# Rows of a half block in a free buffer of attention's weights, and pieces of blocks between the last group's transposes

## The chip, the cores and the metric

The kernel runs on one core of a Trainium2 chip. The metric is the device time of one execution in microseconds. Engines are named as in the profile: PE is TensorE's matmul and PEld its weight load, DVE is VectorE, ACT is ScalarE, POOL is GpSimd, SP is SyncE, which here issues most of the loads.

## The reference

Two layers stand one behind the other. The first is attention that keeps the 32 largest scores of each query; the second sends each token to one of eight experts (a dropless mixture).

```python
# q, k, v: (8, 8, 576, 64)
scores = scale * np.matmul(q, k.transpose(0, 1, 3, 2))
kth = np.partition(scores, -top_k, axis=-1)[..., -top_k:-top_k + 1]   # top_k = 32
scores = np.where(scores >= kth, scores, -1e9)
attn = np.exp(scores - np.max(scores, axis=-1, keepdims=True))
attn = attn / (np.sum(attn, axis=-1, keepdims=True) + 1e-09)
x = np.matmul(attn, v)            # then (B,H,S,D) -> (4608, 512)

logits = x @ w_gate               # (512, 8)
expert_idx = np.argmax(logits, axis=1)
gate_w = softmax(logits)[arange(N), expert_idx]
# tokens sorted by expert; for each expert e with rows lo:hi
h = np.maximum(x_sorted[lo:hi] @ w1[e], 0.0)      # w1: (8, 512, 1024)
y_sorted[lo:hi] = h @ w2[e]                       # w2: (8, 1024, 512)
return gate_w[:, None] * y_sorted[inv_perm]
```

All of it is float32.

## The kernel before

**Attention.** The eight batches come one after the other, each as four pairs of heads. Two neighbouring pairs make nine groups of two query tiles each, so a batch has 18 groups and the kernel 144. For a group, PE multiplies the scores (`products`, L292), ACT copies them out, DVE searches the threshold (`search`), ACT and POOL mask and ACT takes the exponential (`depths`, `less`, `weights`). The result is a tile "w" of 128 partitions by two times 576 numbers, in a pool of three buffers. `transposed` then turns it on PE: four transposes into a PSUM bank "wTm" for each of the group's two tiles (L415), each copied out by ACT to "wT" (L422), and one more "wTl" for the rest (L429), copied to "wTt" (L437). `transposed` is a generator: it stops after the copies and after "wTl", and `loop` puts other work of PE at these stops. For the last group of all, nothing is put there. `outputs` multiplies the turned weights by the values (po, L450), then turns the result into rows and logits (px, L461).

**Routing.** When a batch is done, DVE chooses the experts, PE counts ranks (L531 to L534), and POOL scatters the rows to their expert's place in a DRAM tensor `x_rows` (L567). At the last batch SP and POOL also write blank rows behind the filled ones (`fill_up`, L589), and DVE works out a table that says which block belongs to which expert.

**Blocks.** A block is 128 sorted rows of one expert. `load_rows` fetches its rows to a tile "xg" (L769; four buffers in all, 514 numbers a row: 512 of x, one of the gate, one index), `load_weights` its expert's w1 (L761) and w2 (L763, two buffers each), all on SP's queue. `turned` transposes the rows on PE (xtp, L808), the first layer is 32 matmuls, each of which stands twice in the profile (ph, L913), ACT applies the relu (L918), the second layer is eight matmuls of 512 columns, also twice each (py, L930). ACT scales by the gate (L939), and `put_rows` sends the rows to their tokens in the output by an indirect DMA of POOL (L828), which reads index and gate from the "xg" tile. That store is the last reader of the tile.

A long block has 192 rows: 128 in one "xg" tile and a half of 64 in another (`load_half`, L782). There are four of them, `HALVES`, all in the last part. Their transposes are L798, the first layer is L849, the second L870 (both in PSUM tiles that the program calls "sc"), the turning back of the result L885, and the scaling L889. The rooms for their turned rows and hidden numbers come from the pool "s", attention's scores. A long block's output is turned back and stored in the middle of the next block's first layer (`finish`).

**Order.** A block is cut into 16 pieces: eight of four first-layer matmuls and eight of one second-layer matmul. `pieces(n)` issues the next n of them, going on to the next loaded block where one ends; when a block is begun, `ahead` issues the loads of the one two behind it. Inside `loop` the order on PE, ACT and DVE is the program's own. Three blocks' worth of pieces, `KEEP`, are kept back and issued after the last group, to cover the routing of the last batch. What comes after that, the first two sure blocks, the four long ones and the four plain ones, is ordered by a planner that goes by its own costs; SP's and POOL's queues are ordered by it everywhere.

The end of `loop` before the change, after all 144 groups:

```python
            for _ in turning(len(work) - 1):
                pass
            assert len(late) == 1
            clock = None
            for place in late[0][0]:
                if place == "rows":
                    pieces(4)
            kept = left - (SURE + HALVES + PLAIN) * PIECES
            ...
            pieces(kept)
```

`late[0]` is the ending of the last pair of heads: outputs, routing, tables and loads, in steps.

Of the kernel before, what the change touches and what calls it, by code (L numbers as in the profile page):

```python
# [9 lines left out]
F32 = mybir.dt.float32  # L10
# [20 lines left out]
def _turned(ap: bass.AP, axis: int) -> bass.AP:  # L31
    dims = [list(d) for d in ap.ap]
    step, n = dims[axis]
    dims[axis] = [-step, n]
    return bass.AP(tensor=ap.tensor, offset=ap.offset + step * (n - 1), ap=dims)
# [7 lines left out]
def kernel(  # L43
# [48 lines left out]
    B, U, P, _ = qk.shape  # L92
    N, Dm = out.shape
    S = N // B
# [14 lines left out]
    XW = Dm + 2  # L109
# [20 lines left out]
    k = SimpleNamespace()  # L130

    def open_pools(st, exact):
        for name, bufs in (
            ("load", 2), ("att", 2), ("xp", 1 if exact else 2), ("small", 2),
            ("wp", 1 if exact else 2), ("mlp", 2),
        ):
            setattr(k, name, st.enter_context(tc.tile_pool(name=name, bufs=bufs)))
        for name, bufs in (("ps_s", 2), ("ps_t", 2), ("ps_m", 2)):
            pool = tc.tile_pool(name=name, bufs=bufs, space=bass.MemoryType.PSUM)
            setattr(k, name, st.enter_context(pool))  # L140
        k.exact = exact
        k.apart = False

    def load_unit(b, u, parts=False):
        n = SimpleNamespace(b=b, u=u)
# [107 lines left out]
    def bank(name):  # L253
        return k.ps_t.tile([P, SM], F32, name=name, tag="t")
# [8 lines left out]
    def tails(tiles):  # L263
        return tiles[0][1] == 2 * NC

    def tail_at(n):
        return 0 if n.u % 2 else S
# [140 lines left out]
    def transposed(tiles, w):  # L408

        q = slice(ST + tiles[0][1] * P, ST + (tiles[0][1] + 1) * P)  # L410
        for m, (n, i) in enumerate(tiles):
            pm = bank("wTm")
            for c in range(NC):
                first = c * P + (0 if tails(tiles) else m * ST)
                nc.tensor.transpose(pm[:, c * P:(c + 1) * P], w[:, m, first:first + P], ident)  # L415
            pm4 = pm[:, :].rearrange("p (c q) -> p c q", c=NC)
            if tails(tiles):
                at = tail_at(n)
                pmh = pm4.rearrange("p c (h q) -> p c h q", h=2)
                nc.scalar.copy(wT[:, :, :, at:at + ST], _turned(pmh, 2) if m else pmh)  # L420
            else:
                nc.scalar.copy(wT[:, :, m, q], pm4)  # L422
        yield
        pt = bank("wTl")
        if tails(tiles):
            for a in range(2):
                nc.tensor.transpose(pt[0:ST, a * P:(a + 1) * P], w[:, 1 - a, SM:S], ident)
        else:
            nc.tensor.transpose(pt[:, 0:P], w[:, :, :].rearrange("p m k -> p (m k)")[:, SM:SM + P], ident)  # L429
        yield  # L430
        if tails(tiles):
            pt4 = pt[0:ST, 0:2 * P].rearrange("p (r q) -> p r q", q=ST)
            for h in range(2):
                both = wTt[h * ST:(h + 1) * ST, :].rearrange("p (a q) -> p a q", q=ST)[:, 0:NT + 1:NT, :]
                nc.scalar.copy(both, pt4[:, 0:4:3, :] if h else pt4[:, 1:3, :])
        else:
            nc.scalar.copy(wTt[:, q], pt[:, 0:P])  # L437
# [340 lines left out]

    def load_half(n, piece):
        r = nc.sync.value_load(piece, min_val=0, max_val=EMPTY)  # L780
        n.half = k.mlp.tile([P, 1, XW], F32, name="xg", bufs=4)
        got = nc.sync.dma_start(n.half[0:ST], xv[0:ST, bass.ds(r, 1), :]).ins  # L782
        for put in scattered:
            tc.add_manual_dep(got, put.name, WAIT)
        fetched.append(got)
        return n
# [170 lines left out]
    with fast:  # L957
# [49 lines left out]
        def pieces(n):  # L1007
            nonlocal current, left
            while n > 0 and left > 0:
                if current is None:  # L1010
                    if not landed(loaded[0]):
                        break
                    now = loaded.pop(0)
                    if hasattr(now, "half"):
                        current = long_block(now, following)
                    else:
                        current = block(now, following, stores.append)
                    ahead()
                if clock is None:
                    evacuate()  # L1020
                step = next(current)
                if step == "pause":
                    if clock is not None:
                        break
                    continue
                if step == "last":
                    current = None
                n -= 1
                left -= 1
            return n  # L1030
# [117 lines left out]
        def turning(i):  # L1148
            return transposed(tiles_of(i), w_of.pop(i))
# [9 lines left out]
        def loop():  # L1159
            nonlocal credit, rate, clock  # L1160
            for i in range(min(AHEAD, len(work))):
                multiply(i)
                s_of[i], steps = scores(got_of.pop(i))
                for step in steps:
                    step()
            multiply(AHEAD)
            f_of[0] = fold(s_of[0])
            fold_on(f_of[0])
            for i, (b, g) in enumerate(work):
                tiles = tiles_of(i)  # L1170
                u, tile = g[0]
                if tile == 0 and u % 2 == 0:
                    open_unit(tiles[0][0])
                if tails(tiles):
                    open_unit(tiles[1][0])

                then = lambda: None
                if i + 1 < len(work):
                    f_of[i + 1] = fold(s_of[i + 1])
                    then = lambda: fold_on(f_of[i + 1])  # L1180
                low, nbias, doubts = search(tiles, s_of[i], f_of.pop(i), then)
                at_place("small")
                w_of[i] = depths(s_of[i], low)
                less(s_of.pop(i), w_of[i])
                doubts()
                put_stores()
                scatter(1)
                at_place("pool")
                at_place("relu")
                at_place("rows")  # L1190
                at = i % per_batch
                if at == FIRST and b:
                    rate = level(b) * PIECES / (U * NT)
                credit += rate * len(g)
                room = left
                if b == B - 1 and at >= ARRIVED:
                    room -= KEEP
                    credit = room / (len(work) - i)
                share = {0: 0.5, 1: 1.2, 2: 1.6, 3: 0.5, 2 * NC: 1.4}[tile]
                now = max(0, min(int(credit * share + 0.5), room))  # L1200
                credit -= now
                clock = i
                if i + AHEAD < len(work):
                    s_of[i + AHEAD], steps = scores(got_of.pop(i + AHEAD))
                    for step in steps:
                        step()
                evacuate()
                at_place("turn")
                turns = turning(i - 1) if i else iter(())
                next(turns, None)  # L1210
                part = min(BETWEEN, now - now // 2)
                rest = pieces(part)
                next(turns, None)
                rest = pieces(now - now // 2 - part + rest)
                weights(tiles, w_of[i], nbias)
                next(turns, None)
                evacuate()
                if i + AHEAD + 1 < len(work):
                    multiply(i + AHEAD + 1)
                if tile == NC - 1:  # L1220
                    end = ending(b, u)
                    late.append([end, next(end)])
                at_place("products")
                at_place("weights")
                credit = min(credit + pieces(now // 2 + rest), 6 * rate)

            for _ in turning(len(work) - 1):
                pass
            assert len(late) == 1
            clock = None  # L1230
            for place in late[0][0]:
# [3 lines that stand above are left out]
            assert kept >= 0, kept  # L1235
            k.apart = True
            pieces(kept)
# [20 lines left out]
    with ExitStack() as outer:  # L1258
# [10 lines left out]
        with ExitStack() as st:  # L1269
# [7 lines left out]
            with tc.For_i(0, B, 1) as b:  # L1277
# [3 lines left out]
                for u in range(0, U, 2):  # L1281
# [4 lines left out]
                    for g in groups(u):  # L1286
# [5 lines left out]
                        w = depths(s, low)  # L1292
# [4 lines left out]
                        n, tile = tiles[0]  # L1297
# [76 lines left out]
```

## Time and profile before

| | |
|---|---|
| median of 3 runs | 1328.27 us (1327.86 to 1331.78) |
| the profiled execution | 1330.3 us, its span 1328.6 us |
| busy in the span | PE 1195.5 us (90%), PEld 837.3 (63%), DVE 1073.6 (81%), ACT 933.0 (70%), POOL 657.4 (49%) |
| matmuls of the long blocks (L849, L870) from 1140 to 1314 us | 256 each, 42.8 and 43.4 us busy |
| loads of rows | 37 of 257 KB (L769), 4 of 128.5 KB (L782) |
| loads of expert weights | 74 of 2048 KB |
| granted TensorE clock, 1060 to 1314 us | 1.00 |
| DMA, 1088 to 1156 us and 1156 to 1314 us | share 1.02 at 348 GB/s, and 0.60 at 221 GB/s |

Times in the profile are microseconds from the start of the span. The page divides the span into 40 slices of 33.2 us. A line of the timeline gives the start, the length, the engine and line, what is written and read, and the number of merged instructions; in brackets stands the idle time ahead of it and what ended it. Matmuls follow each other before the one in front has ended, so that the lengths of two neighbours overlap. A line of the waits gives the waiter, what released it, the time in total, the number of waits and the longest. "SPq" is SP's queue.

### The profile page before, as it was taken

What the parts mean: (1) busy time and instruction counts of PE and PEld (TensorE: products, weight loads), DVE (VectorE), ACT (ScalarE), POOL (GpSimd) and SP (SyncE); (2) the same over time, 40 slices, a digit from 0 to 9 for tenths busy, and PEclk for the clock granted to TensorE, in tenths of its full rate; (3) what the DMA queues carried; (4) which work ended last, traced back from release to release, by engine and by line L of the source; (5) the groups of instructions that cost most, each with busy time, mean ns of one, the idle gap of its engine ahead of it and who ended that gap; (6) DMA issues with size and microseconds to landing.
All of it is one profiled execution on the core that took longest, in us unless ns stands there. A gap on an engine that the chain in (4) does not pass through costs nothing. (4 is left out here: it accounts for less than half of the span.)

```text
span 1328.6 us, 24530 instructions
## 1 busy us (share of the span) xinstructions
PE 1195.5 (90%) x7654; PEld 837.3 (63%) x7654; DVE 1073.6 (81%) x4654; ACT 933.0 (70%) x2129; POOL 657.4 (49%) x806
## 2 busy tenths in 40 slices
PE   5767766998889899999999999999999999999995
PEld 3444443666566556676667666766666767799973
DVE  7999999999999999999999999999999942000000
ACT  4888787887898788988888798888878851111210
POOL 2454546564866485647554865576547642000000
PEclk9788788899999899999999999999999999999998
DMA  4000002841293029432954464538354549946780
GB/s 148 30 29 30 30 30 65 311 157 30 72 349 125 30 76 374 172 101 84 367 171 172 137 243 172 173 132 305 134 203 144 208 143 335 347 155 221 291 335 18
DMA packets 98509, 220.95 MB, mean 166 GB/s; under 512 B 5181, under 2 KB 25917, under 8 KB 98368
## 3 DMA queue, kind: packets, MB, share of 16 engines
q1 hardware_dynamic: 91664, 199.02, 42.6%
q0 software_dynamic: 6416, 19.97, 4.2%
q8 instruction: 62, 1.02, 0.3%
q14 instruction: 79, 0.65, 0.1%
q10 hardware_dynamic: 288, 0.30, 0.1%
HBM read 195.88 MB, written 24.17 MB: 166 GB/s over the span
## 5 line engine op out<-in xcount | busy, mean ns | idle before, releaser
L396 POOL TENSOR_TENSOR w<-s,w 128x576 f32<-128x576 f32 x288 | 410.0, 1444 | 417.3 <-ACT w L387 417.3
L913 PE MATMUL ph<-xTs,w 128*128 128x128 f32 x2112 | 260.1, 277 | 3.7 <-ACT xTs L810 3.7
L913 PEld LDWEIGHTS ph<-xTs,w 128*128 128x128 f32 x2112 | 248.7, 192 | 23.2 <-issue 18.6
L930 PE MATMUL py<-w,hT 128*128 128x512 f32 x528 | 250.3, 603 | 2.8 <-ACT hT L918 2.6
L404 ACT ACTIVATE w<-w,nbias 128x576 f32<-128x576 f32 x288 | 224.0, 792 | 4.6 <-POOL w L396 3.9
L387 ACT ACTIVATE w<-s,low 128x576 f32<-128x576 f32 x288 | 207.6, 768 | 4.7
L292 PE MATMUL sc<-qkb 64*128 64x288 f32 (+1 forms) x1280 | 200.0, 463 | 9.5 <-ACT s L299 5.1
L415 PE MATMUL wTm<-turn,w 128*128 128x128 f32 x1152 | 169.4, 287 | 31.9 <-ACT oT L452 14.7
L415 PEld LDWEIGHTS wTm<-turn,w 128*128 128x128 f32 x1152 | 132.0, 145 | 88.3 <-issue 33.4
L299 ACT COPY s<-sc 128x576 f32<-128x576 f32 x288 | 168.7, 639 | 8.3 <-PE sc L292 8.3
L1253 DVE CAST any_i<-pd 1x1 int32<-1x1 f32 x1 | 0.1, 147 | 206.4 <-PE pd L1251 206.4
L354 DVE MAX8 tops<-scr 128x8 f32<-128x168 f32 x576 | 162.9, 317 | 0.0
L422 ACT COPY wT<-wTm 128x512 f32<-128x512 f32 x256 | 139.1, 603 | 23.5 <-PE wTm L415 23.2
L354 DVE MAX8 tops<-few 128x8 f32<-128x144 f32 (+1 forms) x576 | 154.6, 300 | 0.0
L292 PEld LDWEIGHTS sc<-qkb 64*128 64x128 f32 (+1 forms) x1280 | 107.4, 191 | 71.3 <-issue 33.1
L450 PE MATMUL po<-wT,vb 128*64 128x288 f32 x1024 | 149.0, 437 | 0.4 <-ACT wTt L437 0.4
L930 PEld LDWEIGHTS py<-w,hT 128*128 128x128 f32 x528 | 92.7, 193 | 88.4 <-issue 83.8
L828 POOL DMA_INDIRECT out_dram<-y,xg x41 | 41.8, 1020 | 188.3 <-ACT y L889 82.4
L345 DVE MAX8 few<-l 128x8 f32<-128x288 f32 x288 | 127.2, 442 | 0.0
L450 PEld LDWEIGHTS po<-wT,vb 128*64 128x64 f32 x1024 | 72.0, 145 | 72.5 <-issue 22.1
L306 DVE TENSOR_TENSOR h<-s 128x576 f32<-128x576 f32 x144 | 114.0, 792 | 2.6 <-ACT s L299 2.6
L308 DVE TENSOR_TENSOR l<-s 128x576 f32<-128x576 f32 x144 | 110.0, 764 | 0.0
(185 smaller groups left out, 1645.9 us busy)
## 6 DMA issues: line engine op xcount, KB each, us to landing
w<-in_moe_w_dram SPq DMA_DIRECT2D x74, 2048.0 KB
qkb<-in_qk_dram SPq DMA_DIRECT2D x31, 608.0 KB
vb<-in_v_dram SPq DMA_DIRECT2D x32, 320.0 KB
xg<-x_rows SPq DMA_DIRECT2D x37, 257.0 KB
x_rows<-blank SPq DMA_DIRECT2D x13, 257.0 KB
x_rows<-blank POOLq DMA_DIRECT2D x4, 257.0 KB
out_dram<-y,xg POOLq DMA_INDIRECT x41, 2.9
x_rows<-x,posi POOLq DMA_INDIRECT x40, 3.2
```

Of the source, the lines that this page charges most:

```text
L292: nc.tensor.matmul(ps[rows, j, 0:HF], n.q[d, cols], n.k[d, keys], start=True, stop=True)
L299: lambda m=m, ps=ps: nc.scalar.copy(s[:, m, :, :], ps[:, :, 0:HF]) for m, ps in enumerate(got)
L345: nc.vector.max(out=f.few[:, m, QF + 8 * j:QF + 8 * j + 8], in_=away)
L354: nc.vector.max(out=tops[:, m, r * 8:(r + 1) * 8], in_=src[m])
L387: nc.scalar.activation(w[:, m, :], s[:, m, :, :].rearrange("p j k -> p (j k)"), AF.Relu, scale=-STEEP, bias=low[:, m:m + 1],)
L396: k.last_pool = in_turn(nc.gpsimd.tensor_tensor(w[:, m, :], s[:, m, :, :].rearrange("p j k -> p (j k)"), w[:, m, :], op=ALU.subtract)).ins
L404: nc.scalar.activation(w[:, m, :], w[:, m, :], AF.Exp, scale=scale, bias=nbias[:, m:m + 1], accum_out=n.z[:, c:c + 1])
L415: nc.tensor.transpose(pm[:, c * P:(c + 1) * P], w[:, m, first:first + P], ident)
L422: nc.scalar.copy(wT[:, :, m, q], pm4)
L450: nc.tensor.matmul(po[r, 0:HF], n.v[:, c, r], rhs, start=(c == 0), stop=(c == KC - 1))
L913: nc.tensor.matmul(ph[:, f, :], n.w1[:, 0, dt, fc * P:(fc + 1) * P], n.xT[:, dt, :], start=(dt == 0), stop=(dt == DT - 1),)
L930: nc.tensor.matmul(py, hT[:, f, :], n.w2[:, 0, f, :], start=(f == 0), stop=(f == FT - 1))
```

## The change

Two edits, both in the last part. The rows of a half block come into a buffer of the pool of attention's weights "w" (three buffers of 2 times 576 numbers per partition, of which the first 514 are used); before, they came into one of the four "xg" buffers. And in the turning of the last group, one piece of a block is issued at each stop of `transposed`; for this group there is one stop more, behind the copy of the first "wTm", so there are three. These pieces are taken from the same queue of blocks, and what is issued later is as much shorter.

```diff
@@ open_pools
-        k.apart = False
+        k.apart = k.between = False
@@ transposed
             else:
                 nc.scalar.copy(wT[:, :, m, q], pm4)
+                if k.between and not m:
+                    yield
         yield
         pt = bank("wTl")
@@ load_half
         r = nc.sync.value_load(piece, min_val=0, max_val=EMPTY)
-        n.half = k.mlp.tile([P, 1, XW], F32, name="xg", bufs=4)
+        room = k.att.tile([P, 2, S], F32, name="w", bufs=3)[:, :, :].rearrange("p m k -> p (m k)")
+        n.half = room[:, 0:XW].rearrange("p (o w) -> p o w", o=1)
         got = nc.sync.dma_start(n.half[0:ST], xv[0:ST, bass.ds(r, 1), :]).ins
@@ loop
+            k.between = True
             for _ in turning(len(work) - 1):
-                pass
+                pieces(1)
             assert len(late) == 1
             clock = None
```

## The prediction

> **What bounds the kernel now.** I began with the page's slices (each 33.2 us; a digit is the busy share in tenths):
>
> ```profile
> PE   5767766998889899999999999999999999999995
> ...
> DVE  7999999999999999999999999999999942000000
> ```
>
> Until about 1070 us attention's search on DVE is as full as TensorE; from there DVE runs dry and PE alone is full to 1312.9, after which comes a fixed tail of 15.7 us to the span's end at 1328.6. Both edits lie in that last part, so what shortens PE's stream there shortens the kernel one for one. The chain view covers only the end (1299.80 on) and says nothing of this, so next I asked what PE waited for from 1070 on (waiter, line, releaser: us, times, longest):
>
> ```profile
> PE xtp L798 <- DMA xg<-x_rows: 1.7, 4, 0.6
> PE xtp L808 <- DMA xg<-x_rows: 0.7, 1, 0.7
> PE wTm L415 <- ACT wT L422: 0.7, 1, 0.7
> PE wTl L429 <- ACT wT L422: 0.7, 1, 0.7
> PE po L450 <- ACT wTt L437: 0.4, 1, 0.4
> ```
>
> Two clusters: the last group's transposes wait for ScalarE's evacuations, and the long blocks' row transposes wait for their loads. The timeline shows the first (start, length, count, idle before):
>
> ```profile
> 1074.40 1.04 PE L415 MATMUL wTm<-turn,w 128*128 128x128 f32 x8
> ...
> 1078.91 0.66 PE L415 MATMUL wTm<-turn,w 128*128 128x128 f32 x4
> 1080.25 0.66 PE L415 MATMUL wTm<-turn,w 128*128 128x128 f32 x4 [0.68 <-ACT wT L422]
> 1081.58 0.33 PE L429 MATMUL wTl<-turn,w 128*128 128x128 f32 x1 [0.68 <-ACT wT L422]
> 1082.26 2.16 PE L450 MATMUL po<-wT,vb 128*64 128x288 f32 x16 [0.35 <-ACT wTt L437]
> ```
>
> and the second, where the first long block (no wait) stands beside the second:
>
> ```profile
> 1172.27 0.99 PE L798 MATMUL xtp<-turn,xg 128*128 128x128 f32 x8
> 1173.19 10.67 PE L870 MATMUL sc<-s,w 128*128 128x192 f32 x64
> 1183.69 5.36 PE L849 MATMUL sc<-s,w 128*128 128x192 f32 x32
> ...
> 1194.97 0.81 PE L870 MATMUL sc<-s,w 128*128 128x192 f32 x4
> 1196.38 0.66 PE L798 MATMUL xtp<-turn,xg 128*128 128x128 f32 x4 [0.60 <-DMA xg<-x_rows]
> ...
> 1199.23 0.46 PE L798 MATMUL xtp<-turn,xg 64*128 64x64 f32 x4 [0.24 <-DMA xg<-x_rows]
> ```
>
> Why the rows are late is in the waits of SP's queue from 1185 to 1200:
>
> ```profile
> SPq L769 <- DMA out_dram<-y,xg: 43.6, 2, 24.7
> SPq L782 <- DMA out_dram<-y,xg: 2.4, 1, 2.4
> ```
>
> SP stood 24.7 us for a free "xg" buffer, until an old block's output had left it; the load went out at 1193.69 and its transposes began 2.69 us later. Below, A is the block in work at 1079, B to D the kept ones, E and F those before the four long blocks L0 to L3, G the next.
>
> **Part 1: pieces between the last transposes.** It adds no instruction and moves three pieces up. Loss now, start to start: eight wTm take 0.87 us (1074.40, the next matmul at 1075.27), so four take 0.435. 1080.25 - 1078.91 - 0.435 = 0.905 lost; 1081.58 - 1080.25 - 0.435 = 0.895; a lone wTl took 0.10 before matmuls of that kind (1070.86 to 1070.96), so 0.58 before po. In sum 2.38.
>
> What fills it: A has done 14 of its 16 L930 matmuls, so the first piece is its last pair (0.86, 1086.49 to 1087.35), then two pieces of B, whose rows were transposed at 1066.65; eight L913 matmuls take 0.90 (64 of them 7.14: 1103.48 to 1110.62, less a piece's share, 0.89). New order from 1078.91: wTm to 1079.35, piece to 1080.21, wTm at its 1080.25, to 1080.69, piece to 1081.59, wTl to 1081.69, piece to 1082.59, then po, 0.33 later than today but with 2.66 of work done. Gain 2.66 - 0.33 = 2.33. Ends: 1.38 (the idle column 1.71 less the 0.33), and 2.38.
>
> What moves with it. Last outputs and routing start 0.33 later; POOL's chain (L487 to L500), DVE's choice and the scatters shift as much, behind PE's kept work. The four pieces ahead of the ranks stay four; they are now four of B, 3.6 us instead of 3.56. That cover is just enough (the choice ends at 1090.21, its matmul starts at 1090.27), so I put 0 there; without it a late choice costs its lateness. ACT's y of A comes where it came, now without its 0.46 wait for PE; h0 of B is asked for 1.8 us after the px matmuls and done by 2.5, before the Exp of the logits (3.4 after them). On SP, D's loads are issued a little earlier, and w2 of C, which stood for A's last pair until 1087.54, can go at about 1080.3, into a stretch where the DMA engines moved 1 GB/s (1076 to 1088).
>
> **Part 2: halves into "w" buffers.** It removes an "xg" claim from each of L0 to L3; the same 128.5 KB come by the same queue. Loss now against the first long block, whose 64 L870 take 1183.69 - 1173.19 = 10.50 and eight transposes 0.92: L1 runs from 1194.97 to 1207.53, 12.56 for 11.42, so 1.14; L2 from 1218.80 to 1231.41, 12.61, so 1.19; L3 from 1242.68 to 1254.41, 11.73 for 10.96 (four transposes), so 0.77. Sum 3.10. Ends: 2.42, the idle column (0.60 + 0.24 + 0.62 + 0.27 + 0.69), and 3.87, the weight loads' idle column there (0.90 + 0.54 + 0.91 + 0.56 + 0.96). I take 3.10, since the first long block is the nearest row.
>
> What is late next. With four "xg" and rows only, L2's rows take E's buffer (its output issued at 1147.99), L3's F's (1163.03), G's L0's (1190.82, while G's load follows the start of L2 at about 1207): none waits near its use. Three "w" buffers serve L0 to L2 at once, as attention's last transposes end at 1082. L3's half takes L0's and keeps the wait for the store of 1194.34; queued behind it on SP are w1 and w2 of L3 and G's rows. w1 must wait for L1's first half anyhow (1194.97), and is wanted at 1231; 2 MB at the 348 GB/s of 1088 to 1156 take 6 us. So 0. Earlier weights collide with little: from 1156 to 1314 the DMA share is 0.60.
>
> **Sum.** 2.33 + 3.10 = 5.43 us. The profiled execution took 1330.3 (span 1328.6, 1.7 around it): 1324.9. It stands 0.15% above the median of 1328.27, so for that the forecast is 1322.9, 0.41% down. With the low ends (1.38 + 2.42) it is 1324.5, with the high ones (2.38 + 3.87) 1322.0. No change can be told within 0.3%, 4.0 us here, so the bound is 1324.3.
>
> A rule against start-to-start counting: the timeline's wTm ends at 1079.57, the next starts at 1080.25, 0.68 by the column against my 0.905. The Trainium skill, Perfetto Trace Analysis, section on the per-instruction lifecycle (Tensor Engine), says a matmul's end is computed from its size, not observed. So an idle column is no loss either way; summing it, 1.71 + 2.42 = 4.13, would give 1324.1, on the edge of what can be told. Eight in 0.87 us, here, say the column is too small.
>
> **Rivals.**
> 1. *Only the long blocks gain*: the earlier pieces are given back because something before E is late anyway. E and F need rows at 1125.07 and 1139.52. F's are the nearer: issued at 1124.57, behind 15.1 MB, by shapes, queued since 1088 (five weight halves of 2.1, three row blocks and eight blanks of 0.26, scatters 1.2, two stores 0.5), so landed at about 1131.4 by 348 GB/s. Margin 8.1, after the change 5.8. Against it. Time 1325.2.
> 2. *Only the pieces gain*: the order after the loop is a planner's; if it leaves L2's transposes where they are or another wait (the spare rooms of "s") takes their place, 1325.9. For it: L798 sits four matmuls into L870, a planned place. Against: in L0, where rows were there, no time was lost.
> 3. *It does not do what it says*: no piece is to be had at that moment, and halves still wait: 1328.3. Against: one pair of A is left, and B is transposed.
> 4. *Slower*: the last batch's rows. F's load waits for B's store, which POOL runs behind its fills (1113.98), which wait for the scatters' landing (8.8 us); PE now comes 2.3 earlier with three pieces less to cover. Were the scatters held up, by w2 of C and w1 of D now running beside them, F's rows would slip. From a slip of 5.8 PE stands, us for us; 5.4 more eat the gain, and from 15.2 on the kernel is slower by over 0.3%. At a slip of 16 the net is -5.4 + 10.2, so 1333.0. For it: 1088 to 1156 has a DMA share of 1.02. Against: 2.1 MB leave that stretch.
>
> **How the numbers follow.** Both gains 0.70 (1322.0 to 1324.5, nearly all of it beyond the bound); rival 1 0.09, rival 2 0.09, rival 3 0.05, rival 4 0.07. Faster: 0.70 less 0.04 for its slow end, 0.66. Same: 0.04 + 0.09 + 0.09 + 0.05 = 0.27. Slower 0.07. The range takes the forecast's ends and rivals 1 and 2: 1321.9 to 1326.1.
>
> **What would show it.** Right: between the wTm, wTl and po groups near 1079 stand L930 x2 and L913 x8 twice with no idle over 0.1; SP issues w2 near 1080 instead of 1087.54; E's first L913 starts near 1130.1 instead of 1132.38; no L798 or L808 waits for a load, L1 and L2 take 11.4 from the end of their first layer; PE ends near 1307.5. Wrong: SP's rows of L2 still near 1193, PE idle before E, F or L0, or an L870 that waits for ACT.

## The result and the profile after

The changed kernel takes 1322.97 us (median of 6 runs, 1321.82 to 1324.0) against 1328.93 for the kernel before (6 runs, 1327.86 to 1331.78). The ratio is 0.9952, with a 95% interval of 0.9942 to 0.9962. The forecast was 1322.9. In a second set beside other kernels it was 1323.58 against 1329.02, ratio 0.9958 (0.9946 to 0.9970).

The lines of the source have moved: L913 is now L916, L930 L933, L450 L452, L798 L801, L808 L811, L849 L852, L870 L873; the loads L761, L763, L769, L782 are now L763, L765, L771, L785, and the store L828 is L831.

The timeline of PE after, at the last group (start, length, count, idle before):

```profile
1077.54 0.66 PE L415 MATMUL wTm<-turn,w 128*128 128x128 f32 x4
1078.03 1.02 PE L933 MATMUL py<-w,hT 128*128 128x512 f32 x2
1078.89 0.63 PE L415 MATMUL wTm<-turn,w 128*128 128x128 f32 x4
1079.36 1.06 PE L916 MATMUL ph<-xTs,w 128*128 128x128 f32 x8
1080.26 0.27 PE L431 MATMUL wTl<-turn,w 128*128 128x128 f32 x1
1080.37 1.06 PE L916 MATMUL ph<-xTs,w 128*128 128x128 f32 x8
1081.35 2.16 PE L452 MATMUL po<-wT,vb 128*64 128x288 f32 x16
```

A's last pair, then two pieces of B, stand between the transposes, and no bracket is left. The row transposes that stand in a long block turn the rows of the block behind it: those in L1 are L2's. L1 now looks like the first long block:

```profile
1191.38 0.60 PE L801 MATMUL xtp<-turn,xg 128*128 128x128 f32 x4
1191.91 0.46 PE L801 MATMUL xtp<-turn,w 64*128 64x64 f32 x4
1192.30 10.67 PE L873 MATMUL sc<-s,w 128*128 128x192 f32 x64
1202.81 5.36 PE L852 MATMUL sc<-s,w 128*128 128x192 f32 x32
```

From these transposes to the next block it takes 11.43 us, where before it took 12.56, and L1's 64 second-layer matmuls are in one piece. The list of what PE waited for after 1070 us has no line at all.

SP's queue shows how the rows of L2 and L3 come. Before, L2's stood here:

```profile
1193.69 0.35 SPq L769 DMA_DIRECT2D xg<-x_rows  x1
```

After:

```profile
1159.70 2.66 SPq L771 DMA_DIRECT2D xg<-x_rows  x1
1163.13 0.48 SPq L785 DMA_DIRECT2D w<-x_rows  x1
...
1180.93 0.37 SPq L771 DMA_DIRECT2D xg<-x_rows  x1
1193.68 0.48 SPq L785 DMA_DIRECT2D w<-x_rows  x1
```

L2's rows and their half go out at 1159.70 and 1163.13, 28 us and more ahead of their transposes at 1191.38. The rows at 1180.93 are those of L3, out 33 us ahead of their transposes at 1214.08; the half of L3 at 1193.68 is the one load that still waits for an old store (7.6 us in the queue's waits).

Cut at the same matmuls, the two profiled executions compare as follows (us). "L0's row transposes", here and in the expectations below, are those that stand ahead of L0's second layer, at 1172.27 before; the rows that they turn are L1's.

| stretch | before | after | change |
|---|---|---|---|
| start to the last group's first wTm | 1078.91 | 1077.54 | -1.37 |
| first wTm to po | 3.35 | 3.81 | +0.46 |
| po to E's first first-layer matmul | 50.12 | 47.44 | -2.68 |
| from there to L0's row transposes | 39.89 | 39.89 | 0 |
| L0's row transposes to G's first first-layer matmul | 82.14 | 78.94 | -3.20 |
| from there to the last matmul pair | 58.33 | 58.33 | 0 |
| the rest of the span | 15.86 | 15.35 | -0.51 |

The rows that the change touches sum to -5.42. The first and the last row are not its work. Up to the last group PE, DVE and ACT carry the same instructions in the same order in both programs, and POOL the same ones, and in the twelve profiles of this study that stretch ends anywhere from 1076.64 (a variant of the kernel before) to 1078.91 (the kernel before); the rest of the span lies between 15.3 and 15.9 in them.

Below, "the first stretch" is that from the last group's first wTm to E's first first-layer matmul (53.47 before, 51.25 after) and "the long stretch" that from L0's row transposes to G's first first-layer matmul (82.14 and 78.94).

### The profile page after: what moved, and what is told of

The parts are those of the page before. It is cut to its first block, busy times and chain, and to the rows that moved or that the text cites. A ratio compares the mean times of both kernels' runs of the same rounds, so it can differ in the third digit from the quotient of the medians.

```text
span 1321.3 us, 24526 instructions
## 1 busy us (share of the span) xinstructions
PE 1194.3 (90%) x7654; PEld 838.0 (63%) x7654; DVE 1072.6 (81%) x4654; ACT 932.3 (71%) x2129; POOL 660.2 (50%) x806
## 5 line engine op out<-in xcount | busy, mean ns | idle before, releaser
L916 PE MATMUL ph<-xTs,w 128*128 128x128 f32 x2112 | 261.2, 277 | 3.6 <-ACT xTs L813 3.6
L916 PEld LDWEIGHTS ph<-xTs,w 128*128 128x128 f32 x2112 | 249.6, 193 | 22.7 <-issue 18.0
L933 PE MATMUL py<-w,hT 128*128 128x512 f32 x528 | 249.6, 602 | 3.9 <-ACT hT L921 3.7
L933 PEld LDWEIGHTS py<-w,hT 128*128 128x128 f32 x528 | 92.4, 192 | 89.4 <-issue 83.5
L452 PE MATMUL po<-wT,vb 128*64 128x288 f32 x1024 | 148.1, 435 | 0.0
L831 POOL DMA_INDIRECT out_dram<-y,xg x37 | 38.1, 1030 | 171.4 <-ACT y L892 76.5
L452 PEld LDWEIGHTS po<-wT,vb 128*64 128x64 f32 x1024 | 71.9, 145 | 71.8 <-issue 21.5
```

The lines of the kernel that those rows point to most:

```text
L452: nc.tensor.matmul(po[r, 0:HF], n.v[:, c, r], rhs, start=(c == 0), stop=(c == KC - 1))
L916: nc.tensor.matmul(ph[:, f, :], n.w1[:, 0, dt, fc * P:(fc + 1) * P], n.xT[:, dt, :], start=(dt == 0), stop=(dt == DT - 1),)
L933: nc.tensor.matmul(py, hT[:, f, :], n.w2[:, 0, f, :], start=(f == 0), stop=(f == FT - 1))
```

## Experiments

**Each part alone.** The first kernel keeps the "w" buffers and issues no pieces; the second has the pieces and puts the halves back into "xg":

```diff
 # halves alone
-            k.between = True
             for _ in turning(len(work) - 1):
-                pieces(1)
+                pass
 # pieces alone
-        room = k.att.tile([P, 2, S], F32, name="w", bufs=3)[:, :, :].rearrange("p m k -> p (m k)")
-        n.half = room[:, 0:XW].rearrange("p (o w) -> p o w", o=1)
+        n.half = k.mlp.tile([P, 1, XW], F32, name="xg", bufs=4)
```

Expected of the halves alone:

> Only the halves go to "w" buffers; nothing stands between the last group's transposes. Theory A (PE's late row transposes are the cost): from the first row transpose of L0 to G's first L913, 82.14 us before and 78.94 after, it takes 78.9 to 79.0; the last group's wTm, wTl and po keep their gaps of about 0.9, 0.9 and 0.6 us; time 3.1 to 3.2 us below before, ratio 0.9976. Rival B (the earlier w2 of C and the emptier DMA stretch behind it help everything after): the long blocks keep part of their loss and the ratio stays above 0.999. Rival C (the weights queued behind the rows are the cost) expects the same 0.9976 as A and is told apart elsewhere.

Expected of the pieces alone:

> Only the pieces between the last group's transposes; the halves claim "xg" buffers as before. Theory A: from the last group's first wTm to E's first L913, 53.47 us before and 51.25 after, it takes 51.2 to 51.3; the long blocks keep their waits for rows, 82.1 us from L0's row transposes to G's first L913; time 2.2 to 2.3 us below before, ratio 0.9983. Rival B (DMA relief spreads): the long blocks lose part of their waits too, 80 to 81 us, and the ratio comes near 0.996. If the two parts do not add up, the sum of this one's gain and that of the halves alone misses the whole change's by over 1 us.

Expected of the changed kernel beside them:

> The changed kernel once more beside its two parts, for the sum: 5.4 us below before by start-to-start times of the two stretches (2.2 and 3.2), ratio 0.9959. If instead the 1.37 us by which the last group began earlier in the two profiles shown, and the 0.5 us in the tail, belong to the change, the ratio comes to 0.9945.

Measured against 1329.02 for the kernel before: halves alone 1324.95, ratio 0.9970 (0.9959 to 0.9981); pieces alone 1327.69, ratio 0.9989 (0.9980 to 0.9997); the whole change 1323.58, ratio 0.9958 (0.9946 to 0.9970). The parts sum to 4.07 + 1.33 = 5.40 us, the whole is 5.44: they add up, within intervals that are some 1.5 us wide to each side for the halves, so that an agreement to 0.04 us is luck. The long stretch settles the halves: 78.94 with the halves alone, as in the whole change, and 82.46 with the pieces alone. So the late rows cost 3.2 to 3.5 us, and rival B's spreading relief is not there.

The first stretch held two surprises. With the pieces alone it was 52.14, and in the second profile of the changed kernel 51.76, not 51.25. That profile has one line for PE's waits after 1070 us, at E's first first-layer matmul:

```profile
PE ph L916 <- DMA w<-in_moe_w_dram: 0.3, 1, 0.3
```

PE stood there for w1 of E, 0.5 us start to start (at 6.87 us for D's second layer, as elsewhere, E's first matmul was due at 1128.51, and it begins at 1129.02). In the profile of the pieces alone the same matmul begins 0.88 late; there the page puts the wait down to ACT's y, which ended at that moment. The landings tell that it was the same load. The trace keeps sixteen semaphore updates for each of these loads, and the last is taken here as its landing: w1 of E landed at 1128.88 in the one profile and at 1130.23 in the other, 0.14 and 0.13 us ahead of the late matmul.

The second surprise was in the halves alone, where the first stretch was 55.16, longer than before. These are its busy times and its granted clock (the number behind POOL's) around the gaps:

```profile
core 0: us, PE busy (x) PEld busy (x) DVE busy (x) ACT busy (x) POOL busy (x), PEclk, DMA share, GB/s
1078.00:1082.00 4.00, 2.29 (x17) 1.19 (x15) 0.00 (x0) 1.59 (x4) 0.00 (x0) 1.00 0.00 0
1082.00:1086.00 4.00, 4.00 (x20) 1.85 (x20) 0.22 (x1) 0.54 (x4) 0.00 (x0) 0.58 0.00 0
```

and the po matmuls behind the gaps:

```profile
1081.90 3.40 PE L452 MATMUL po<-wT,vb 128*64 128x288 f32 x16 [0.35 <-ACT wTt L439]
1085.08 1.16 PE L452 MATMUL po<-wTt,vb 128*64 128x288 f32 x4
```

Sixteen po matmuls took 3.18 us to the next group where they take 1.99 in the kernel before: the clock had been taken down. To see whether this belongs to that kernel, it and the kernel before were profiled again.

> The kernel before, once more, for what a second profile of the same program shows. Theory A: the last group's gaps are again 0.9, 0.9 and 0.6 us, the long blocks' stretch 82.1 to 82.6 us; the first wTm of the last group comes anywhere between 1076.6 and 1079.0 us, since programs that are the same up to there already differed by that. On the clock: the profile with the halves alone had a granted clock of 0.66 and 0.50 from 1082 to 1086, behind the three gaps, which made the po matmuls 1.7 us longer, while two other profiles with these gaps stayed at 1.00. If the gaps set it off by chance, this one may show either; if it belongs to that kernel, never this one.

> The kernel with the halves alone, once more. If the drop of the clock behind the last group's gaps comes by chance, the stretch from the first wTm to E's first L916 is 53.5 us at a clock of 1.00 or about 55.2 with a drop; if it belongs to this kernel, 55.2 again. The long blocks take 78.9 to 79.0 us either way.

Both ran the stretch at a clock of 1.00, in 53.47 us each, with long stretches of 82.46 and 78.94; the times of the two runs were 1329.11 and 1325.87. So of five profiles that have all three gaps, one shows the drop, and a second profile of that same program does not. It cost 1.69 us where it came. No profile with pieces in the three gaps shows it; there are six, too few to say that it can't come there.

**Rows or the weights behind them.** In the kernel before, SP's queue held L2's weights back behind its late rows (1197.39 and 1198.02, though their buffers had come free at 1172 and 1184). For L2 and L3, the third and fourth long block, the order was turned round (`longs_in` starts as an empty list):

```diff
                 elif isinstance(piece, list):
-                    rows_in = load_half(load_rows(SimpleNamespace(), piece[0]), piece[1])
+                    longs_in.append(piece)
+                    if len(longs_in) > 2:
+                        rows_in = load_weights(SimpleNamespace(), expert)
+                        loaded.append(load_half(load_rows(rows_in, piece[0]), piece[1]))
+                        loaded[-1].at = clock
+                        continue
                     rows_in = load_half(load_rows(SimpleNamespace(), piece[0]), piece[1])
```

> The kernel before with one order changed: for the third and fourth long block, L2 and L3, SP issues w1 and w2 ahead of the rows and the half, which keep their "xg" buffers and their waits. Theory A (PE lost its time to late rows): SP issues w1 of L2 near 1173 and w2 near 1184 instead of 1197 and 1198, the rows stay near 1193 and 1196, L798 keeps its waits, the stretch from L0's row transposes to G's first L913 stays 82.1 us, and the time is that of before, ratio 1.000. Theory C (the weights behind the rows were the cost): the stretch falls to 79 to 80 us, ratio 0.998.

The weights of L2 went out at 1170.20 and 1181.62, and the waits stayed, as these lines of PE's timeline show:

```profile
1192.70 0.81 PE L870 MATMUL sc<-s,w 128*128 128x192 f32 x4
1194.19 0.66 PE L798 MATMUL xtp<-turn,xg 128*128 128x128 f32 x4 [0.68 <-DMA xg<-x_rows]
1194.69 2.12 PE L870 MATMUL sc<-s,w 128*128 128x192 f32 x12
1196.96 0.46 PE L798 MATMUL xtp<-turn,xg 64*128 64x64 f32 x4 [0.16 <-DMA xg<-x_rows]
```

The long stretch is 82.60, the time 1329.44 against 1328.86, ratio 1.0006 (0.9997 to 1.0015). With the weights out 16 to 27 us earlier the stretch gained nothing: the rows alone were late.

**Two pieces instead of three.** The extra stop is taken away, so that the first gap stays open:

```diff
-            k.between = True
             for _ in turning(len(work) - 1):
                 pieces(1)
```

> The changed kernel without the extra stop behind the first wTm: two pieces instead of three, at the old stops. Theory A (the gain is the idle that is filled): the first gap of 0.9 us is back, the other two are filled, po starts 3.7 us after the first wTm, and the stretch from the first wTm to E's first L913 is 1.4 us under the 53.47 of before, 52.05, if w1 of E is in time. Theory B (the gain is A's last pair early, which frees w2's buffer for the load of C's into an empty DMA stretch): that pair still comes early, SP's w2 goes out near 1080, and the stretch is that of three pieces, 51.25 to 51.8.

```profile
1077.61 0.66 PE L415 MATMUL wTm<-turn,w 128*128 128x128 f32 x4
1078.94 0.66 PE L415 MATMUL wTm<-turn,w 128*128 128x128 f32 x4 [0.68 <-ACT wT L422]
1079.44 1.02 PE L933 MATMUL py<-w,hT 128*128 128x512 f32 x2
1080.30 0.31 PE L431 MATMUL wTl<-turn,w 128*128 128x128 f32 x1
```

The gap of 0.90 (1.33 less four transposes' 0.435) is back, po starts 3.82 us after the first wTm, w2 of C still goes out early (1080.49), and the first stretch is 52.16, with no wait at E. One piece less costs 0.9 us: the gain is the idle that is filled, not the earlier load. This kernel ran once, in 1324.03 us.

**What stands next.** One more piece, where the px matmuls wait for ScalarE's copy:

```diff
+            seen = 0
             for place in late[0][0]:
+                seen += place == "products"
                 if place == "rows":
                     pieces(4)
+                elif place == "products" and seen == 2:
+                    pieces(1)
```

> The changed kernel with one more piece of B, put between the last po and the px matmuls, where PE still loses 0.4 us to ScalarE's copy of oT (ten px matmuls take 1.65 us there, 1.23 in an earlier unit). Theory A: the px matmuls start 0.9 us after po's end with no loss, E's first L913 comes 0.4 us earlier, counted from the last group's first wTm (50.85 for 51.25), and the ranks keep four pieces ahead of them; time 0.4 us below the changed kernel, ratio to before 0.9956. Rival: the routing chain is what counts here and the 0.5 us by which px is later comes back as a wait of the ranks or of E: 51.25 or more.

This was a miss: 1324.03 us, ratio 0.9964 (0.9952 to 0.9976), and a first stretch of 52.42. The ten px matmuls did shrink to 1.23, but the planner now put A's store ahead of the logits on POOL, the scatters began 0.6 later after the first wTm, and E waited for its weights:

```profile
PE ph L916 <- DMA w<-in_moe_w_dram: 1.3, 1, 1.3
```

In all the profiles up to here w1 of E is issued behind SP's four blank fills, which wait for the scatters. From that issue to PE's late start it took 15.9 us here (1113.76 to 1129.66) and 16.3 in the changed kernel's second profile (1112.69 to 1129.02). So the load was put ahead of the fills:

```diff
                 assert len(loaded) == 2
+                load_w1(ready, firsts[0][0])
                 fill_up()
```

(`load_w1` is the first half of `load_weights`, which then loads w2 alone.) The same was done with the extra piece.

> The changed kernel with one order changed on SP: w1 of E is issued ahead of SP's four blank fills instead of behind them. Theory D: w1 of E is what now stands next behind the pieces' gain. In three profiles with the pieces PE waited 0.35, 0.7 and 1.3 us at E's first L913 matmul, and the stretch from the last group's first wTm to that matmul took 51.76, 52.14 and 52.42 us where 51.25 is free of waits. By D the load goes out near 1108 instead of 1112, lands some 4 us or more earlier, no wait stands at E, the stretch is 51.2 to 51.3, and the time is 0 to 0.5 us below the changed kernel, ratio to before 0.9955. Rival (the wait is a matter of the DMA engines' total work up to E, not of this load's place): the wait at E stays between 0.3 and 1.3 us.

> The same with one more piece of B ahead of the px matmuls, which alone gave 52.42 us from the last group's first wTm to E's first first-layer matmul, 1.3 of it a wait for w1 of E. Theory D: with that load out earlier the extra piece pays: no wait at E, 50.85 us, and 0.4 below the kernel without the extra piece, ratio to before 0.995. Rival: what was lost there comes from the routing, whose POOL steps were set back 0.4 us behind a store; then the wait at E stays and the stretch is above 51.3.

In SP's timeline of the first of these kernels the load stands ahead of the fills (L778 is its load of rows, L763 that of w1):

```profile
1106.99 0.35 SPq L778 DMA_DIRECT2D xg<-x_rows  x1
1108.11 0.37 SPq L763 DMA_DIRECT2D w<-in_moe_w_dram  x1
1109.28 4.06 SPq L591 DMA_DIRECT2D x_rows<-blank  x4
```

Neither kernel has a wait of PE left after 1070 us. The first stretch is 51.25 without and 50.93 with the extra piece, so the piece that lost 0.66 against the second profile of the changed kernel now gains 0.32. The landings of w1 of E (us):

| profile | issued | landed | E's first matmul |
|---|---|---|---|
| the kernel before | 1113.81 | 1130.97 | 1132.38 |
| the kernel before, again | 1112.40 | 1130.43 | 1131.25 |
| the changed kernel | 1112.28 | 1128.42 | 1128.79 |
| the changed kernel, second profile | 1112.69 | 1128.88 | 1129.02 |
| pieces alone | 1113.63 | 1130.23 | 1130.36 |
| one more piece | 1113.76 | 1129.53 | 1129.66 |
| load ahead of the fills | 1108.11 | 1124.03 | 1129.67 |
| the same, one more piece | 1107.39 | 1122.94 | 1128.48 |

Where PE began late, it began 0.13 to 0.14 us behind the landing. With the load ahead of the fills 5.5 us and more are to spare. The rival is out: A's store still stands ahead of the logits in the last kernel, and its scatters begin 15.78 us after the first wTm, where they began 15.79 after it in the kernel with the late load. So theory D holds, the place of that one load was what ate the gain. The times are 1323.82, ratio 0.9956 (0.9942 to 0.9970), and 1322.88, ratio 0.9954 (0.9940 to 0.9967). Neither can be told from the changed kernel (0.9952 and 0.9958) by time; what the load's place gives shows in the stretches and landings alone.

## Why the prediction was right, and where it was not

**The sum.** Forecast 2.33 + 3.10 = 5.43; the profile gives 2.22 + 3.20 = 5.42. Both terms were counted from start to start and each was right to about 0.1 us; that their misses cancel is luck. Luck also helped the time: 1322.9 was set on 1328.27 for the kernel before, which took 1328.93 beside the changed one, so that the gain there is 5.96, and 5.44 in the second set. And 2.22 is the better of the changed kernel's two profiles; the other has 1.71. The idle column, 4.13, was too small, as the text held against it: the Trainium skill, Perfetto Trace Analysis, section on the per-instruction lifecycle (Tensor Engine), calls the end of a matmul an estimate. Here the column shows 1.3 us less than the 5.4 that were gained. The low end for the pieces, 1.38, takes po's delay off an idle time that is already net of it; the term that goes with the column is 1.71.

**Part 1.** The gaps and what fills them were as told. po came 0.46 later instead of 0.33: each change between transposes and pieces costs a few hundredths that a steady pitch doesn't show (0.49 from the first wTm to the piece, counted as 0.435). The cover ahead of the ranks held: the choice ends at 1089.30, its matmul starts at 1089.35. w2 of C went out 1.55 us after the first wTm, forecast 1.4.

**The step that failed is in rival 1**: it asked what else is late ahead of E, named F's rows as the nearest, and priced their landing as the bytes queued since 1088 over 348 GB/s, which left a margin of 5.8 us after the change. The nearest was w1 of E, which the text never placed. Before, it landed at 1130.97 for a use at 1132.38: 1.4 us, and 0.8 to 2.5 us in the other four profiles without pieces, mostly less than the gain itself. So the part's gain is 2.22 in one profile with three pieces, 1.71 and 1.33 in two others, and 1.05 in the one with a fourth piece, all with the load in its old place. The chance of 0.09 was for the wrong load, but the mechanism was real and partly at work.

Naming that load would not have been enough, since the price was wrong too. By the text's shapes about 12.5 MB stood in the queue from 1088 up to and with w1 of E, which at 348 GB/s would land it near 1124 (an estimate); it landed 7 us later. The engines moved 261 GB/s from 1114 to 1120 at a share of 1.07, and w2 of E went out at 1118.12, 13 us before w1 had landed; no run parts these two. F's rows show the same: the text had them land 8.1 us ahead of their use in the kernel before, and in its second profile they landed at 1136.49 for a use at 1138.39, 1.9 ahead. In the changed kernel POOL stored B at 1101.05, ahead of the fills and not behind them as at 1113.98, and F's rows went out at 1115.77 instead of 1124.57. This order is the planner's and was not foreseen. Still they landed only 1.4 us ahead of their use (1134.51 and 1135.93), not 5.8.

**Part 2.** Right in mechanism and size. L1, L2 and L3 gained 1.13, 1.19 and 0.89; only the last was put too low (0.77), since four transposes and 64 matmuls take 10.84 rather than 10.96. L3's half kept its wait and nobody felt it, as the text said. Rival 2 had one thing right, that the place of L798 inside L870 was planned: with the rows early the planner put the transposes in front.

**Rivals 3 and 4.** Three pieces were to be had. F's rows were not late in any profile, but 0.6 to 0.7 us from it in three of them. The emptier stretch that the text set against rival 4 hardly helped: from the end of the last scatter to POOL's first fill it took 8.85 us before and 8.60 after (POOL's wait in the list is 5.27 only because B's store now stands in between). The lateness that rival 4 feared for F's rows came for E's weights, by 1.5 us at most (one more piece), far from its deciding point.

**Cases.** "Faster" at 0.66 came true: 0.9952 and 0.9958, both beyond the 0.3% that were the bound, though the second interval's end, 0.9970, touches it.

## What to carry to other kernels

Price an idle gap by the starts of neighbouring matmuls against a steady run of the same kind, and check a second block of the same shape that doesn't wait: that gave 2.33 for 2.22 and 3.10 for 3.20. When work is pulled ahead of a path, list every operand of the first consumer behind it, weights as well as rows, with issue and landing; a margin that equals the gain will give some of it back. Read the landing from the trace: bytes over a mean rate put it 7 us too early here. Where a load waits for a store to free its buffer, a buffer that an earlier stage has left is a cheap way out.

## What the runs showed of the hardware that was not expected

**Short gaps can cost the clock.** Three gaps that sum to 2.4 us, with PE busy for 2.29 of 4 us by the profile, took the granted clock to 0.58 over the next 4 us in one profile of five, for 1.69 us. The Trainium skill, TensorE: Matmul & The Clock Gate, Part 1, has a free-running window of about 3.4 us after which an idle PE is throttled to half. The trace agrees with the window and its length: the clock was at half from 1082.66 to 1086.07, 3.41 us, and in each of the five profiles with the gaps all switches of the granted clock lie on a grid of 3.41 us that starts elsewhere in each. The window ahead of the drop, 1079.25 to 1082.66, holds 2.12 us of the gaps, counted by the pitch of the transposes; the window with the most of them in the other four holds 2.04, 1.80, 1.69 and 1.65. So PE was not idle through the window that brought the drop, and the place of the window fits the one in five. With 2.04 on the one side and 2.12 on the other, and a single drop, this is not shown, and where the bound lies stays open.

**A load's issue can take microseconds.** Issuing one load of rows on SP took 0.35 us with idle DMA engines (1193.69 before) and 8.41 us in the changed kernel at 1115.77, 9.58 at most (one more piece, 1116.63), all while the engines were full; whatever stands behind it on SP starts that much later. Full engines alone are not the reason: at a share above 1 the rows at 1106.71 and the weights at 1112.28 and 1114.53 took 0.35 to 0.41 us. What sets it apart was not looked for. The same 2 MB that need 6 us at 348 GB/s landed 14.6 to 18.0 us after their issue (w1 of E, ten profiles); in the changed kernel's second profile the engines moved 5.0 MB in the 16.3 us from issue to use, at 307 GB/s.

**Programs that are the same up to there start their last part up to 2.3 us apart** (1076.64 and 1078.91; the kernel before itself at 1078.91 and 1077.78), so that a term below 1 us is read from a stretch of the trace and not from the time.
